# Global part of the values product in two 64-row tiles, its values masked within a head group, and batch 1's first transposes in the score pair

## The chip, the cores and the metric

The kernel runs on one core of a Trainium2 chip. The core has five engines that run side by side, each with its own queue of instructions in program order: TensorE (PE; its weight loads are listed as PEld), VectorE (DVE), ScalarE (ACT), GpSimd (POOL) and SyncE (SP). SP and POOL issue most of the DMAs; sixteen DMA engines carry them out. [...] The metric is the device time of one execution in microseconds, as the median of several runs.

## The reference

Attention with a band and eight global positions, on 8 batches, 8 heads, 576 positions and 64 elements a head, then a gated feed-forward block on the 4608 resulting tokens.

```python
def _attn_ref(q, k, v, global_idx):
    scores = scale * np.matmul(q, k.transpose(0, 1, 3, 2))
    pos = np.arange(S)
    mask = np.abs(pos[:, None] - pos[None, :]) <= window      # window = 32
    is_global[global_idx] = True                              # 8 positions
    mask = mask | is_global[:, None] | is_global[None, :]
    scores = np.where(mask, scores, -1000000000.0)
    attn = softmax(scores)
    return np.matmul(attn, v)
...
def _moe_ref(x, w_gate, w_val, w_out):
    g = x @ w_gate
    silu = g * (1.0 / (1.0 + np.exp(-g)))
    return (silu * (x @ w_val)) @ w_out
```

Here x is the attention output with the heads side by side (4608 x 512), the gate and value weights are 512 x 1536, the output weights 1536 x 512.

## The kernel before

**Attention of one batch.** It is a row of steps, all within `attention(b)`. `step_T` (lines 363 to 387; batch 0 has its own, `step_T0`) transposes k and q of a pair of heads with PE into one PSUM pair and copies them to kT and qT; batches 3 and up get kT and qT from DMA transposes on SP instead, whose sources are bf16 copies made by POOL's casting DMAs (`cast_qk`, tiles kf and qf). `step_GT` transposes the gathered, masked rows of the global positions. `step_S2` and `step_SG` make the scores of the global queries against all keys and of all queries against the global keys; the latter, exponentiated and masked, are the tile pg: 128 partitions, 16 for each head, by 576 positions. `step_P2T` transposes the global queries' probabilities to p2t: with PE and an ACT copy up to batch 3, with a DMA transpose on SP from batch 4 on (line 448). `step_AV2` (line 458) multiplies them with the values va. Its result has, in every partition, two heads' columns (66 wide: 64 values, the sum and a low part); DVE spreads it with the mask dmask into the tile gv, in which each of the eight heads has its columns and only that head's partitions are not zero (lines 468 to 480).

`step_S` (line 482) makes banded scores: matmuls with 64 rows (one head) and 128 columns, two of them, in different row halves of the array, into two banks. ACT exponentiates, DVE multiplies with the band. `step_AV` (line 532) adds up, for 128 positions, a group of four heads in each of two banks: for each group first the global part, two matmuls with all 128 partitions of pg as rows, 64 positions as columns each, and the 264 columns of gv of that group (line 546), then eight windowed matmuls with 64 columns (line 555) on va and on its shifted copy vb, a DMA on SP. `normalise` on DVE divides, and `step_X` transposes the result into xT. `step_AV8` (line 566) does the same for the last 64 positions, both groups in one bank.

**The feed-forward block** works in nine chunks of 512 tokens. Each chunk has twelve gates (eight 128x128 matmuls of 512 columns each, then tanh on ACT and two products on DVE, gv and h) and four output steps (twelve matmuls each, a copy on ACT, a DMA out). These 16 units per chunk set the order: every step of attention is hung behind a unit by hand (`gaps`), batch b + 1 beside the units of chunk b for most of the kernel, and each engine executes in that order.

**PSUM** has eight banks: the score pair (pool psc, tag "sc", two banks), a second pair (pool pm, tag "m") and four single banks (pool pf) for gates and outputs. A pair is handed over only when its last reader is done. Gate 2 of chunk 0 also takes the pair "m" (pgv).

Batch 1's `step_T(0)` stands behind gate 2 of chunk 0, `step_T(1)` behind gate 3 (after batch 0's `step_AV8`), `step_T(2)` behind gate 4, `step_GT` and `step_T(3)` behind gate 5. In batches 3 to 7 the list of steps is spread over a chunk's units: score step 1 stands behind gate 6, score step 2 and `step_AV2` behind gate 8, score step 3 and `step_AV(0)` behind gate 9, score step 4 and `step_AV(2)` behind an output step, `step_AV(3)` and `step_AV8` behind a later one.

Of the kernel before, what the change touches and what calls it, by code (L numbers as in the profile page):

```python
# [9 lines left out]
FP32 = mybir.dt.float32  # L10
BF16 = mybir.dt.bfloat16
# [3 lines left out]
ALU = mybir.AluOpType  # L15
AX = mybir.AxisListType

P = 128


def bc(ap, dims):

    return bass.AP(tensor=ap.tensor, offset=ap.offset, ap=[ap.ap[0]] + dims)
# [3 lines left out]
def kernel(  # L27
# [11 lines left out]
    nc = tc.nc  # L39

    B, H, S, D = q.shape
# [8 lines left out]
    HP = H // 2  # L50
# [6 lines left out]
    W = D + 2  # L57
# [4 lines left out]
    const = ctx.enter_context(tc.tile_pool(name="const", bufs=1))  # L62
# [3 lines left out]
    bp = ctx.enter_context(tc.tile_pool(name="bp", bufs=2))  # L66
    gw = ctx.enter_context(tc.tile_pool(name="gw", bufs=2))
    work = ctx.enter_context(tc.tile_pool(name="work", bufs=2))
# [3 lines left out]
    psc = ctx.enter_context(tc.tile_pool(name="psc", bufs=1, space=bass.MemoryType.PSUM))  # L72
    pm = ctx.enter_context(tc.tile_pool(name="pm", bufs=1, space=bass.MemoryType.PSUM))
# [97 lines left out]
    def clear(i):  # L171
        nc.vector.memset(kT_bufs[i][:, :, 0:WIN], 0.0)
        nc.vector.memset(kT_bufs[i][:, :, WIN + S : KC], 0.0)
        nc.vector.memset(va_bufs[i][:, :, :, D : D + 2], 0.0)
        nc.vector.memset(va_bufs[i][:, :, :, D : D + 1], 1.0)
        nc.vector.memset(va_bufs[i][0:WIN, 0, :, :], 0.0)
        nc.vector.memset(va_bufs[i][P - WIN : P, 4, :, :], 0.0)
# [4 lines left out]
        out=oh16.rearrange("p h a r -> p (h a r)"),  # L182
# [4 lines left out]
        out=p8, in_=ident.rearrange("p (a g) -> p g a", g=NG), axis=AX.X, op=ALU.add  # L187
    )
    dmask = const.tile([P, HP, 2], FP32)
    gofs = const.tile([P, B], I32)  # L190

    nc.vector.tensor_tensor(out=dmask, in0=oh16[:, :, 0, :], in1=oh16[:, :, 1, :], op=ALU.add)
    clear(0)
    tmp8h = const.tile([P, NG], FP32)
    hrow = const.tile([P, 1], FP32)
    nc.vector.tensor_tensor(
        out=tmp8h, in0=dmask.rearrange("p h r -> p (h r)"), in1=i8_f, op=ALU.mult
# [4 lines left out]
        out=gidx_f, in_=gidx_i64.bitcast(I32).rearrange("p (a b) -> p a b", b=2)[:, :, 0]  # L202
# [8 lines left out]
        out=hrow, in0=hrow, scalar1=float(S), scalar2=gcol, op0=ALU.mult, op1=ALU.add  # L211
# [4 lines left out]
        out=mka, in_=oh16.rearrange("p h a r -> p a r h"), axis=AX.X, op=ALU.add  # L216
# [6 lines left out]
        out=thr, in0=asel, scalar1=R2 + 0.25, scalar2=-0.25, op0=ALU.mult, op1=ALU.add  # L223
# [114 lines left out]
    def attention(b):  # L338
        kT = kT_bufs[b % 2]
        va = va_bufs[b % 2]  # L340
        st = {}
# [21 lines left out]
        def step_T(hp):  # L363
            if hp == 0:
                qTs[b] = bp.tile([P, HP, S], BF16, tag="qT", name="qT")
            pool, tag = (pm, "m") if (hp in (0, 2) if b == 1 else hp == 3) else (psc, "sc")
            pair = pool.tile([P, 2, 1024], BF16, tag=tag, name="ps_t")
            pss = []
            for n, name in enumerate(("k", "q")):
                ps = pair[:, n, 0:S].rearrange("p (j i) -> p j i", j=LJ)  # L370
                pss.append(ps)
                src = loaded[b][name]
                for j in range(LJ):
                    for par in range(2):
                        nc.tensor.transpose(  # L375
                            out=ps[64 * par : 64 * par + 64, j, :],
                            in_=src[:, 2 * hp + par, D * j : D * (j + 1)],
                            identity=ident[0:LP, 0:LP],
                        )
            nc.scalar.copy(  # L380
                out=kT[:, hp, WIN : WIN + S].rearrange("p (i j) -> p i j", j=LJ),
                in_=pss[0].rearrange("p j i -> p i j"),
            )
            (nc.scalar.copy if hp % 2 else nc.vector.tensor_copy)(
                out=qTs[b][:, hp, :].rearrange("p (i j) -> p i j", j=LJ),
                in_=pss[1].rearrange("p j i -> p i j"),
            )
# [70 lines left out]
        def step_AV2():  # L458
            ps = mtile([P, 2, W], FP32, "ps_av2")
            for u in range(5):  # L460
                for hp in range(HP):
                    nc.tensor.matmul(
                        out=ps[32 * hp : 32 * hp + 32, :, :],
                        lhsT=st["p2t"][:, u, 32 * hp : 32 * hp + 32],
                        rhs=va[:, u, 2 * hp : 2 * hp + 2, :],
                        start=(u == 0), stop=(u == 4), skip_group_check=True,
                    )
            gv = bp.tile([P, HP, 2, W], BF16, tag="gv", name="gvt")
            nc.vector.tensor_tensor(  # L469
                out=gv, in0=bc(ps, [[0, HP], [W, 2], [1, W]]),  # L470
                in1=bc(dmask, [[2, HP], [1, 2], [0, W]]), op=ALU.mult,
            )
            lo = work.tile([P, HP, 2], FP32, tag="lo", name="lo")
            nc.vector.tensor_tensor(
                out=lo, in0=bc(ps[:, :, D : D + 1], [[0, HP], [W, 2]]), in1=dmask, op=ALU.mult
            )
            nc.vector.tensor_tensor(  # L477
                out=gv[:, :, :, D + 1], in0=lo, in1=gv[:, :, :, D], op=ALU.subtract
            )
            st["gv"] = gv  # L480
# [53 lines left out]
        def step_AV(tp):  # L534
            st["xa", tp] = work.tile([P, H, D], BF16, tag="xa", name="xa", bufs=3)
            if b == 0:
                pool, tag = (pm, "m") if tp % 2 else (psc, "sc")
            elif b < XQ:
                pool, tag = (psc, "sc") if tp and (b < XB or tp % 2) else (pm, "m")
            else:  # L540
                pool, tag = pm, "m"
            full = pool.tile([P, 2, 512], FP32, tag=tag, name="ps_av")
            ps = full[:, :, 0 : 4 * W].rearrange("p g (h c) -> p g h c", c=W)
            for hg in range(2):
                for e in range(2):
                    nc.tensor.matmul(  # L546
                        out=ps[64 * e : 64 * e + 64, hg],
                        lhsT=st["pg"][:, P * tp + 64 * e : P * tp + 64 * e + 64],
                        rhs=st["gv"].rearrange("p h r c -> p (h r) c")[:, 4 * hg : 4 * hg + 4, :],
                        start=True, stop=False, skip_group_check=True,  # L550
                    )
                pt = st["p", 2 * (tp // 2) + hg]
                for hl in range(4):
                    for e in range(2):
                        nc.tensor.matmul(  # L555
                            out=ps[64 * e : 64 * e + 64, hg, hl, :],
                            lhsT=pt[:, hl % 2, 4 * (hl // 2) + 2 * (tp % 2) + e, :],
                            rhs=(va if e == 0 else st["vb"])[:, tp, 4 * hg + hl, :],
                            start=False, stop=(hl == 3), skip_group_check=True,
                        )  # L560
            if b == 0:
                st["xa*", tp] = lambda: normalise(ps, st["xa", tp], 8)
            else:
                normalise(ps, st["xa", tp], 8)

        def step_AV8():
            pt = st["p", 4]
            if b >= XQ:
                full = psc.tile([P, 2, 512], FP32, tag="sc", name="ps_av8")
                ps = full[:, 0, 0 : 4 * W].rearrange("p (h c) -> p h c", c=W)  # L570
            else:
                ps = mtile([P, 4, W], FP32, "ps_av8")
            for hg in range(2):
                nc.tensor.matmul(
                    out=ps[64 * hg : 64 * hg + 64], lhsT=st["pg"][:, 512:576],
                    rhs=st["gv"].rearrange("p h r c -> p (h r) c")[:, 4 * hg : 4 * hg + 4, :],
                    start=True, stop=False, skip_group_check=True,
                )
            for hl in range(4):
                for hg in range(2):  # L580
                    h = 4 * hg + hl
                    nc.tensor.matmul(
                        out=ps[64 * hg : 64 * hg + 64, hl, :],
                        lhsT=pt[:, h % 2, h // 2, :], rhs=va[:, 4, h, :],
                        start=False, stop=(hl == 3), skip_group_check=True,
                    )
            st["xa8"] = work.tile([P, 4, D], BF16, tag="xa8", name="xa8")
            normalise(ps, st["xa8"], 4)
# [87 lines left out]
        if b < XQ:  # L676
# [7 lines left out]
            [L(step_S2), L(step_SG)],  # L684
            [L(step_S, 0), L(step_P2T)],
            [],
            [L(step_S, 1)],
            [L(step_S, 2), L(step_AV2)],
            [L(step_S, 3), L(step_AV, 0), L(step_X, 0)],
            [L(step_AV, 1), L(step_X, 1)],  # L690
            [L(step_S, 4), L(step_AV, 2), L(step_X, 2)],
# [187 lines left out]
```

The softmax here doesn't subtract the row's maximum and nothing guards it: scores larger than these inputs give would overflow.

## Time and profile before

| what | value |
|---|---|
| median of 6 runs | 370.38 us (367.71 to 371.48) |
| the profiled execution | 368.02 us |
| its span, first to last instruction | 366.3 us |
| PE clock granted, mean | 1.000 |
| L546 PE, global part of AV, 128x264 on 64 columns, x128 | 18.0 us busy, 295 ns each |
| L555 PE, windowed part, 128x66 on 64 columns, x512 | 35.4 us busy, 198 ns each |
| L493 PE, banded scores, 64x64 on 128 columns, x576 | 16.2 us busy, 196 ns each |
| L574 PE, global part of AV 8, x16 | 2.3 us busy, 284 ns each |
| L469 DVE, mask product gvt, 128x528, x8 | 5.6 us busy, 701 ns each |
| L448 SP, DMA transpose p2t, x4, issue to landing | 2.7 / 6.3 / 9.6 us (least, median, most) |

The span is that of one profiled execution on the core; its time includes 1.7 us before and after it. Busy time of PE counts pipelined matmuls that overlap, and their ends are modelled: how long a stretch of PE takes is read from the starts of its matmuls, not from their durations. A few matmul records are missing from the trace. A wait is put down to the engine whose event came last.

### The profile page before, as it was taken

Reading aid. Unit: us, or ns where it says so; the run is one execution under the profiler, and the core shown is the slowest. Engines: PE = TensorE matmul, PEld = TensorE weight load, DVE = VectorE, ACT = ScalarE, POOL = GpSimd, SP = SyncE. Lnnn points to the kernel's source line nnn. Section 1 sums busy time; section 2 is a strip of 40 time slices with the busy share of each in tenths; the row PEclk is TensorE's granted clock in tenths of the full one; section 3 lists DMA queues with packets and bytes.
Section 4 is the critical chain, followed back from the end, with each engine's and each line's share of the span. In section 5 each row is a group of like instructions: output and inputs, shape, how many; then the busy total and the mean of one; then the engine's idle time right before and its main releaser. Section 6 shows DMA issues by size and latency. Waiting matters only on the chain.

```text
span 366.3 us, 7940 instructions
## 1 busy us (share of the span) xinstructions
PE 345.7 (94%) x3237; PEld 175.2 (48%) x3290; DVE 235.7 (64%) x469; ACT 152.8 (42%) x237; POOL 96.7 (26%) x114
## 2 busy tenths in 40 slices
PE   3876999999999999999999999999999999999996
PEld 2554545554544454444444454444544454444444
DVE  6674787268944885488548854886388728824850
ACT  5634673467323552355225532552354323323322
POOL 7934545924444001450246013100000000000000
PEclk9999999999999999999999999999999999999999
DMA  7999999999999926999999999941340131011002
GB/s 104 143 215 204 125 201 195 184 197 142 152 174 159 181 55 113 117 153 158 151 137 142 157 124 146 180 66 53 108 100 2 43 113 27 0 57 60 0 9 108
DMA packets 141637, 43.52 MB, mean 119 GB/s; under 512 B 126368, under 2 KB 135840, under 8 KB 141600
## 3 DMA queue, kind: packets, MB, share of 16 engines
q0 software_dynamic: 93824, 19.40, 66.1%
q1 hardware_dynamic: 47776, 23.60, 31.2%
q8 instruction: 26, 0.43, 0.5%
q14 instruction: 11, 0.09, 0.1%
HBM read 38.28 MB, written 15.34 MB: 146 GB/s over the span
## 4 chain that ended last, share of the span: by engine, by line
PE 84%; DMA 6%; POOL 3%; DVE 3%; ACT 2%; issue 1%; POOLq 0%; DVEq 0%
PE po L772 25%; PE pg L711 24%; PE pv L711 23%; DMA kg<-in_k_dram,gofs 3%; DMA wg_sb<-in_moe_w_gate_dram 3%; PE ps_av L546 3%; PE ps_s L493 3%; PE ps_av L555 2%; ACT pe L501 1%; POOL va L102 1%; PE ps_t L375 1%; DVE pt L507 1%; DVE gvt L469 1%; PE ps_s L427 1%; PE po L759 1%
## 5 line engine op out<-in xcount | busy, mean ns | idle before, releaser
L711 PE MATMUL pg<-xT,wg_sb 128*128 128x512 bf16 x391 | 106.1, 380 | 1.9 <-issue 0.2
L711 PE MATMUL pv<-xT,wv_sb 128*128 128x512 bf16 x410 | 105.9, 379 | 0.2
L744 DVE SCALAR_TENSOR_TENSOR gv<-th,pg 128x512 bf16<-128x512 bf16 x107 | 73.2, 685 | 39.5 <-ACT th L742 38.8
L742 ACT ACTIVATE th<-pg 128x512 bf16<-128x512 f32 x107 | 63.9, 598 | 80.4 <-PE pg L711 76.3
L772 PE MATMUL po<-wo_sb,h 128*128 128x512 bf16 x409 | 92.6, 379 | 1.4 <-issue 1.0
L748 DVE TENSOR_TENSOR h<-gv,pv 128x512 bf16<-128x512 bf16 x107 | 73.5, 687 | 11.5 <-PE pg L711 0.5
L711 PEld LDWEIGHTS <-wv_sb 128*128 128x128 bf16 x424 | 41.5, 98 | 50.0
L772 PEld LDWEIGHTS <-h 128*128 128x128 bf16 x420 | 39.9, 98 | 46.4
L102 POOL DMA_DIRECT2D va<-in_v_dram x40 | 35.2, 976 | 97.3 <-PE ps_av L555 74.5
L711 PEld LDWEIGHTS <-wg_sb 128*128 128x128 bf16 x424 | 37.0, 98 | 40.9 <-issue 1.7
L777 ACT ACTIVATE osb<-po 128x512 f32<-128x512 f32 x35 | 20.9, 597 | 81.7 <-PE po L772 74.9
L501 ACT ACTIVATE pe<-ps_s 128x1024 bf16<-128x1024 f32 (+1 forms) x40 | 37.5, 938 | 18.7 <-PE ps_s L493 17.9
L507 DVE TENSOR_TENSOR pt<-pe,band 128x1024 bf16<-128x1024 bf16 (+1 forms) x40 | 25.4, 635 | 20.4 <-ACT pe L501 20.4
L522 DVE TENSOR_REDUCE den<-ps_av 128x8 f32<-128x16 f32 (+1 forms) x40 | 6.7, 167 | 35.6 <-PE ps_av L555 33.4
L528 DVE TENSOR_TENSOR xa<-ps_av,den 128x512 bf16<-128x512 f32 (+1 forms) x40 | 25.5, 638 | 1.7 <-DMA xT<-xa 0.3
L493 PEld LDWEIGHTS <-kT 64*128 64x128 bf16 x576 | 11.3, 98 | 15.9 <-issue 14.8
L546 PE MATMUL ps_av<-gvt,pg 128*64 128x264 bf16 x128 | 18.0, 295 | 0.9 <-DVE gvt L477 0.9
L555 PE MATMUL ps_av<-vb,pt 128*64 128x66 bf16 x256 | 17.7, 198 | 0.0
L555 PE MATMUL ps_av<-va,pt 128*64 128x66 bf16 x256 | 17.7, 198 | 0.0
L555 PEld LDWEIGHTS <-pt 128*64 128x64 bf16 x512 | 17.6, 114 | 0.2
L493 PE MATMUL ps_s<-qT,kT 64*128 64x64 bf16 x576 | 16.2, 196 | 1.1 <-ACT pe L501 1.1
L109 POOL DMA_DIRECT2D qf<-in_q_dram x5 | 14.0, 2804 | 0.0
(122 smaller groups left out, 220.9 us busy)
## 6 DMA issues: line engine op xcount, KB each, us to landing
out_dram<-osb SPq DMA_DIRECT2D x35, 256.0 KB, 2.1
vb<-va SPq DMA_DIRECT2D x14, 264.0 KB, 5.1
va<-in_v_dram POOLq DMA_DIRECT2D x24, 128.0 KB, 5.7
kf<-in_k_dram POOLq DMA_DIRECT2D x5, 576.0 KB, 11.6
qf<-in_q_dram POOLq DMA_DIRECT2D x5, 576.0 KB, 18.2
k_bf<-in_k_dram POOLq DMA_DIRECT2D x6, 288.0 KB, 13.6
q_bf<-in_q_dram POOLq DMA_DIRECT2D x6, 288.0 KB, 14.4
va<-in_v_dram POOLq DMA_DIRECT2D x16, 96.0 KB, 5.6
```

Source lines behind the costliest of these rows:

```text
L102: nc.gpsimd.dma_start(out=va[lo:hi, u, :, 0:D], in_=vs[t0 + lo : t0 + hi])
L493: nc.tensor.matmul(out=ps[:, par, 64 * slot : 64 * slot + 64], lhsT=kT[r : r + 64, hp, 64 * t : 64 * t + P], rhs=qTs[b][r : r + 64, hp, 64 ...
L501: nc.scalar.activation(out=pe, in_=ps[:, :, 0 : 64 * ns].rearrange("p r (s c) -> p r s c", c=64), func=AF.Exp, scale=SCALE,)
L507: mult = lambda: nc.vector.tensor_tensor(out=pt.rearrange("p r s c -> p (r s) c"), in0=pe.rearrange("p r s c -> p (r s) c"), in1=bc(band, ...
L528: nc.vector.tensor_tensor(out=xa.rearrange("p (g h) d -> p g h d", g=g), in0=bc(ps, pst + [[1, D]]), in1=bc(den, [[4, g], [1, 4], [0, D]]) ...
L546: nc.tensor.matmul(out=ps[64 * e : 64 * e + 64, hg], lhsT=st["pg"][:, P * tp + 64 * e : P * tp + 64 * e + 64], rhs=st["gv"].rearrange("p h ...
L555: nc.tensor.matmul(out=ps[64 * e : 64 * e + 64, hg, hl, :], lhsT=pt[:, hl % 2, 4 * (hl // 2) + 2 * (tp % 2) + e, :], rhs=(va if e == 0 els ...
L711: nc.tensor.matmul(out=ps[:, 0:n], lhsT=w[:, cc, P * fc : P * (fc + 1)], rhs=xT[:, cc, t0 : t0 + n], start=(cc == 0), stop=(cc == NCC - 1),)
L742: nc.scalar.activation(out=th[:, 0:n], in_=pg[:, 0:n], func=AF.Tanh, scale=0.5)
L744: nc.vector.scalar_tensor_tensor(out=gv[:, 0:n], in0=th[:, 0:n], scalar=1.0, in1=pg[:, 0:n], op0=ALU.add, op1=ALU.mult,)
L748: nc.vector.tensor_tensor(out=st["h"][:, fc, 0:n], in0=gv[:, 0:n], in1=pv[:, 0:n], op=ALU.mult)
L772: nc.tensor.matmul(out=po, lhsT=st["h"][:, fc, P * ts : P * (ts + 1)], rhs=wo_sb[:, fc, :], start=(fc == 0), stop=(fc == NFC - 1),)
```

## The change

The global part of the values product is split by head groups instead of by positions. Partitions 0 to 63 of pg belong to heads 0 to 3, partitions 64 to 127 to heads 4 to 7. One matmul for each group now takes its 64 partitions as rows and all 128 positions as columns; the two lie in different row halves and write different banks. gv is masked only within a group: it holds four heads' columns instead of eight, with a mask dmh that is made once at the start from dmask. In `step_AV` both global matmuls now come first, and the windowed matmuls of both groups after them. In `step_AV8` the two global matmuls take 64 rows and 64 columns each and write one bank, at different partitions.

Batch 1's `step_T(0)` takes the score pair instead of the pair "m", and its copy of q is made by ACT instead of DVE. In batches 3 to 7 `step_AV2` moves from behind score step 2 to behind score step 1.

```diff
@@ -190,6 +190,8 @@
     nc.vector.tensor_tensor(out=dmask, in0=oh16[:, :, 0, :], in1=oh16[:, :, 1, :], op=ALU.add)
+    dmh = const.tile([P, 2, 2], FP32)
+    nc.vector.tensor_tensor(out=dmh, in0=dmask[:, 0:2], in1=dmask[:, 2:4], op=ALU.add)
     clear(0)
@@ -363,7 +365,7 @@
-            pool, tag = (pm, "m") if (hp in (0, 2) if b == 1 else hp == 3) else (psc, "sc")
+            pool, tag = (pm, "m") if hp == (2 if b == 1 else 3) else (psc, "sc")
@@ -381,7 +383,7 @@
-            (nc.scalar.copy if hp % 2 else nc.vector.tensor_copy)(
+            (nc.scalar.copy if hp % 2 or (b == 1 and hp == 0) else nc.vector.tensor_copy)(
@@ -465,14 +467,14 @@
-            gv = bp.tile([P, HP, 2, W], BF16, tag="gv", name="gvt")
+            gv = bp.tile([P, 2, 2, W], BF16, tag="gv", name="gvt")
             nc.vector.tensor_tensor(
-                out=gv, in0=bc(ps, [[0, HP], [W, 2], [1, W]]),
-                in1=bc(dmask, [[2, HP], [1, 2], [0, W]]), op=ALU.mult,
-            )
-            lo = work.tile([P, HP, 2], FP32, tag="lo", name="lo")
+                out=gv, in0=bc(ps, [[0, 2], [W, 2], [1, W]]),
+                in1=bc(dmh, [[2, 2], [1, 2], [0, W]]), op=ALU.mult,
+            )
+            lo = work.tile([P, 2, 2], FP32, tag="lo", name="lo")
             nc.vector.tensor_tensor(
-                out=lo, in0=bc(ps[:, :, D : D + 1], [[0, HP], [W, 2]]), in1=dmask, op=ALU.mult
+                out=lo, in0=bc(ps[:, :, D : D + 1], [[0, 2], [W, 2]]), in1=dmh, op=ALU.mult
             )
@@ -542,13 +544,13 @@
             for hg in range(2):
-                for e in range(2):
-                    nc.tensor.matmul(
-                        out=ps[64 * e : 64 * e + 64, hg],
-                        lhsT=st["pg"][:, P * tp + 64 * e : P * tp + 64 * e + 64],
-                        rhs=st["gv"].rearrange("p h r c -> p (h r) c")[:, 4 * hg : 4 * hg + 4, :],
-                        start=True, stop=False, skip_group_check=True,
-                    )
+                r = slice(64 * hg, 64 * hg + 64)
+                nc.tensor.matmul(
+                    out=ps[:, hg], lhsT=st["pg"][r, P * tp : P * tp + P],
+                    rhs=st["gv"][r].rearrange("p h r c -> p (h r) c"),
+                    start=True, stop=False, skip_group_check=True,
+                )
+            for hg in range(2):
                 pt = st["p", 2 * (tp // 2) + hg]
@@ -572,8 +574,8 @@
             for hg in range(2):
                 nc.tensor.matmul(
-                    out=ps[64 * hg : 64 * hg + 64], lhsT=st["pg"][:, 512:576],
-                    rhs=st["gv"].rearrange("p h r c -> p (h r) c")[:, 4 * hg : 4 * hg + 4, :],
+                    out=ps[64 * hg : 64 * hg + 64], lhsT=st["pg"][64 * hg : 64 * hg + 64, 512:576],
+                    rhs=st["gv"][64 * hg : 64 * hg + 64].rearrange("p h r c -> p (h r) c"),
                     start=True, stop=False, skip_group_check=True,
                 )
@@ -684,8 +686,8 @@
             [],
-            [L(step_S, 1)],
-            [L(step_S, 2), L(step_AV2)],
+            [L(step_S, 1), L(step_AV2)],
+            [L(step_S, 2)],
             [L(step_S, 3), L(step_AV, 0), L(step_X, 0)],
```

## The prediction

> **What bounds the kernel now.** First the head of the page and its table of busy time: one engine sets the end.
>
> ```profile
> span 366.3 us, 7940 instructions
> PE 345.7 (94%) x3237; PEld 175.2 (48%) x3290; DVE 235.7 (64%) x469; ACT 152.8 (42%) x237; POOL 96.7 (26%) x114
> ```
>
> TensorE (PE) is busy for 94% of the span, and the chain that ended last is 84% PE. From about 36 us on its matmuls follow one another almost without a hole, so whatever PE is given or spared there moves the end one for one. VectorE (DVE, 64%) and ScalarE (ACT, 42%) have room. The change must then be read in three places: PE's own time in a step, the few waits of PE, and transfers that PE would meet earlier. Second, the list of waits; PE has few that this change touches:
>
> ```profile
> PE ps_t L375 <- DVE h L748: 2.5, 1, 2.5
> ...
> PE ps_av L546 <- DVE gvt L477: 0.9, 5, 0.2
> ```
>
> Once, 2.5 us: the first transposes of batch 1 wait for h of gate 2, which shares their PSUM pair. Five times, 0.2 us each: the global part of AV 0, in batches 3 to 7, waits for the masked values. Third, the timeline of PE around one AV step (start, duration):
>
> ```profile
> 253.06 0.30 PE L546 MATMUL ps_av<-gvt,pg 128*64 128x264 bf16 x2
> 253.20 0.19 PE L555 MATMUL ps_av<-va,pt 128*64 128x66 bf16 x1
> ...
> 253.33 0.28 PE L546 MATMUL ps_av<-gvt,pg 128*64 128x264 bf16 x2
> 253.44 0.19 PE L555 MATMUL ps_av<-va,pt 128*64 128x66 bf16 x1
> ...
> 253.54 0.19 PE L555 MATMUL ps_av<-vb,pt 128*64 128x66 bf16 x1
> 253.67 0.39 PE L772 MATMUL po<-wo_sb,h 128*128 128x512 bf16 x1
> ```
>
> Durations overlap, so starts are what to read. A pair of 64-column global matmuls costs 0.11 us (253.33 to 253.44) and runs side by side; right after a change of tile shape the same pair costs 0.14 (253.06 to 253.20). Eight windowed matmuls (four pairs) take 0.13. The last pair, 0.03, is followed by 0.10 of nothing before the 128x128 matmul at 253.67: that is a **change of shape**. It shows again here:
>
> ```profile
> 256.36 0.29 PE L493 MATMUL ps_s<-qT,kT 64*128 64x64 bf16 x8
> 256.58 0.30 PE L546 MATMUL ps_av<-gvt,pg 128*64 128x264 bf16 x2
> ...
> 247.44 0.41 PE L493 MATMUL ps_s<-qT,kT 64*128 64x64 bf16 x16
> 248.04 0.30 PE L546 MATMUL ps_av<-gvt,pg 128*64 128x264 bf16 x2 [0.19 <-DVE gvt L477]
> ...
> 169.74 0.41 PE L493 MATMUL ps_s<-qT,kT 64*128 64x64 bf16 x16
> 170.08 0.47 PE L462 MATMUL ps_av<-va,p2t 128*32 128x132 bf16 x20
> ```
>
> Score matmuls have just the shape that the change gives the global part: 64 rows, 128 columns, two at a time into two banks. Eight of them to the next step take 0.22, sixteen take 0.34 (169.74 to 170.08): so four pairs cost 0.12, one pair 0.03, which is the time of one matmul alone (264 columns take 0.11, so 64 take 0.03), and the rest of 0.22, 0.10, is the change of shape. The sixteen before AV 0 take 0.60 instead of 0.34: there PE really waits 0.26.
>
> **The change, part by part** (plus is gained).
>
> *1. Transposes of batch 1.* Gate 2's eight matmuls end at 32.40 (31.54 and four of 0.216). Step T 0 could start at 32.50; it starts at 35.08. In the score pair its last user is score step 4 of batch 0, read by an ACT exp at 30.85 to 31.45: no wait left. T 1 now follows in the same pair and must wait for T 0's two copies, both on ACT: first copy 0.74 after T 0's start (as now, 35.08 to 35.82), then 0.64 and 0.65, done near 34.5; PE reaches T 1 after T 0 (0.63), gate 3 (1.73) and AV 8 (0.23), near 35.1. Hidden, by 0.6. The ACT copy also holds up gate 3's tanh by some 0.1, hidden because gate 4 uses other banks. So 2.58 is won at 32.5, and the stall goes to what is late next: transfers, which do not come earlier.
>
> ```profile
> 40.87 0.39 POOL L247 TENSOR_TENSOR kqm<-qg,mka 128x128 bf16<-128x128 f32 x1
> 46.70 0.46 SPq L130 DMA_DIRECT2D vb<-va  x1
> DMA to landing us min/median/max: 7.6/7.6/7.6
> ```
>
> The gathered rows of batch 1 are masked until 41.26, so step GT, now at 42.74, cannot start before 41.3: 1.4 remains. The shifted values vb of batch 1, issued at 46.70, land 7.6 later, at 54.30; their first use in AV 0 is at 55.55 and becomes 54.35 at best: 1.20 remains. The new mask dmh adds one DVE operation (dmask's row: 0.16) ahead of the clears and of the gather's offsets, for which POOL waits; in the first 40 us the DMA engines are full, so I let landings slip by 0.15. **+1.05** (bounds: 0, if the loads are later still; 2.58, if they are earlier).
>
> *2. AV steps.* Removed: one global pair, 0.11, and the 0.03 of the first pair after a change. Added: a change of shape between the two parts, 0.10, and about 0.01 of refill, as score steps show. Net +0.03 each; AV 1 to 3 of batch 1 and four in each of batches 2 to 7, 27 in all, **+0.81**; AV 0 of batch 1, waiting for vb, saves its second pair, **+0.11**. Bounds per step: +0.06 if refills cost nothing, -0.08 if the row pair runs in series.
>
> *3. Score step straight before AV.* Both now have one shape: the change in front goes, 0.10. AV 0 and AV 2 of batches 3 to 7, AV 0 of batch 2: 11 times, **+1.10**. Bound below: 0.
>
> *4. Masked values ready earlier.* AV 2 (step_AV2) moves from score step 2 to score step 1, two gates earlier (it issues no DMA), so AV 0's wait goes: 5 x 0.26, **+1.30**. The smaller mask product saves DVE 0.27 (701 ns for 528 columns; 424 for 256 in xa), off the path. Behind it on DVE stand gate 7's products; two gates later there is one product less before score step 3's. No loss.
>
> *5. AV 8.* Its two matmuls become 64x64 tiles.
>
> ```profile
> 262.95 0.19 PE L555 MATMUL ps_av<-vb,pt 128*64 128x66 bf16 x1
> 262.98 0.28 PE L574 MATMUL ps_av<-gvt,pg 128*64 128x264 bf16 x2
> 263.09 0.29 PE L582 MATMUL ps_av<-va,pt 128*64 128x66 bf16 x8
> ```
>
> Today there is no change of shape on either side; two come in, 0.20 in batches 3 to 7, and 0.08 net in batches 1 and 2, where a gate precedes: **-1.16**. No 64x64 tile is in this trace: above, 0 if it is no change of shape; below, a further 0.11 for each of seven if the two run in series. I take the middle: all other shape changes cost the same, and all other tile pairs run together.
> [...]
>
> *6. The new wait.* AV 2 reads p2t, for batches 4 to 7 a DMA transpose. Moved two gates up, it meets the landing.
>
> ```profile
> 157.80 2.78 SPq L448 DMA_TRANSPOSE p2t<-p  x1
> DMA to landing us min/median/max: 9.6/9.6/9.6
> ...
> 165.84 0.41 PE L493 MATMUL ps_s<-qT,kT 64*128 64x64 bf16 x16
> ```
>
> Batch 4: issued 157.80, landed 167.40; score step 1 starts at 165.84, AV 2 would start 0.34 later, at 166.18: **1.27 of waiting**. Batch 5 in the same way: issued 195.46, 9.1 to landing, 204.56; score step 1 at 203.40, AV 2 at 203.74: 0.87, both with 0.05 for the semaphore (h of gate 2 ends at 35.03, PE starts at 35.08). Batches 6 and 7 land after 2.7 and 3.4 us, over 4 us early. What differs is the cast of a later batch's k (issued 155.03, landing 11.6 later), which runs beside the first two. PE is in order: behind the waiting matmul stand gate 7 and, on DVE, the mask product and gate 7's products; nobody else is late. Cast and transpose both hang on AV 8 of the batch before, so the distance keeps. **-2.14** (bounds: 0 if landing takes 8.3; -4 more if it takes two us longer each time).
> [...]
>
> **Sum:** 1.05 + 0.81 + 0.11 + 1.10 + 1.30 - 1.16 - 2.14 = +1.07. The profiled execution took 368.02 us (span 366.3 and 1.7 around it); the median shown is 370.38. So 366.95 for a run like the profiled one, and 369.3 for the median.
>
> **Rivals.** *A, no wait for p2t:* the transpose lands in time in most executions. For it: 1.3 us of earlier landing is enough, and 6 and 7 have far more. Against: both congested batches agree within 0.5. Gain 3.2, 367.2 us. *B, slower: the two row tiles run one after the other.* Each of 27 + 7 steps loses 0.11: 1.07 - 3.74 = -2.7, 373.1 us. It decides from 0.03 per pair (no gain left) and costs over 0.5% from 0.09. Against it stand the score pairs at 0.03 a pair. *C, p2t later:* with 11.6 instead of 9.6 in both batches, -4 more: 373.3 us; the old place was 2.6 and 3.0 from landing, so nothing in the trace shows more. *D, step 1 brings nothing*, since loads come later in slower executions: 370.4, inside "no change".
>
> **Numbers.** About 0.5% (1.85 us) is what can be told from no change. Forecast 0.60, A 0.25, B 0.07, C 0.08. Forecast alone: 368.0 to 371.2; of its 0.60, 0.05 gains over 0.5% (step 1 whole). So faster 0.30, same 0.55, slower 0.15. The range for 8 in 10 takes in A and the near part of C: 367.1 to 371.6.
>
> **What would show it.** Right: T 0 near 32.5 and holes before GT and the first vb; AV steps of 0.57 with one pair of 64x128 globals and a 0.10 gap behind it; no gap between scores and globals; holes of about 1.3 and 0.9 before AV 2 of batches 4 and 5, none in 6 and 7. Wrong: global starts 0.11 apart (B), no holes (A), or larger ones (C).

## The result, and the profile after

| | before | after |
|---|---|---|
| median | 369.6 us (74 runs, 367.49 to 375.37) | 367.15 us (37 runs, 365.38 to 370.01) |
| ratio | | 0.9936, 95% interval 0.9921 to 0.9952 |
| the profiled execution, its span | 368.02, 366.3 us | 366.57, 364.8 us |

The change makes the kernel faster by 0.64%, 2.4 us (1.8 to 2.9). Predicted was 369.3 us (367.1 to 371.6) from a gain of 1.07, "no change" the likeliest. The time lies in the range, but only 0.05 above its lower end, in part because the median before came out at 369.6, not at the 370.38 that the forecast started from (0.9936 of that is 368.0). The sign of the sum was right; its size was less than half, and by the forecast's own line of 0.5% the outcome is "faster", which had 0.30, not "no change", which had 0.55. The two profiles differ by 1.45 us, near the sum; the medians differ by more. That second difference is the case's question.

The head of the page and the waits of PE (engine, line, engine waited for; us in total, times, longest), after:

```profile
span 364.8 us, 7818 instructions
PE 346.6 (95%) x3177; PEld 170.8 (47%) x3226; DVE 233.7 (64%) x469; ACT 153.3 (42%) x238; POOL 97.4 (27%) x114
...
PE ps_av L464 <- DMA p2t<-p: 1.0, 2, 0.8
PE ps_g L395 <- POOL kqm L249: 0.8, 1, 0.8
```

PE sets the end as before (78% of the chain that ended last, 84% before). Both old waits are gone from the list (T 0 for h, AV 0 for the masked values); the two that take their place are those of the sum, for p2t and for the masked rows.

The timeline of all engines around the first transposes of batch 1 (start, duration, idle time in front and what ended it), after:

```profile
32.23 0.45 PE L377 MATMUL ps_t<-ident,k_bf 96*64 96x96 bf16 x12
...
40.84 0.40 POOL L249 TENSOR_TENSOR kqm<-qg,mka 128x128 bf16<-128x128 f32 x1
40.93 0.59 PE L395 MATMUL ps_g<-ident,kqm 128*128 128x128 bf16 x2 [0.77 <-POOL kqm L249]
...
54.32 0.22 PE L557 MATMUL ps_av<-vb,pt 128*64 128x66 bf16 x1
```

T 0 starts 2.85 us earlier (35.08 before). GT then waits 0.77 for the masked rows, and the first use of vb, 54.32 instead of 55.55, comes as its transfer lands (issued at 46.20, landed 8.08 later). 1.23 us are kept.

The timeline of PE around score step 3, AV 3 and AV 8 of batch 6, after:

```profile
246.47 0.41 PE L495 MATMUL ps_s<-qT,kT 64*128 64x64 bf16 x16
246.72 0.28 PE L548 MATMUL ps_av<-gvt,pg 64*128 64x264 bf16 x2
...
251.72 0.29 PE L548 MATMUL ps_av<-gvt,pg 64*128 64x264 bf16 x2
251.94 0.22 PE L557 MATMUL ps_av<-va,pt 128*64 128x66 bf16 x1
251.99 0.20 PE L557 MATMUL ps_av<-va,pt 128*64 128x66 bf16 x1
...
252.19 0.19 PE L557 MATMUL ps_av<-vb,pt 128*64 128x66 bf16 x1
252.32 0.39 PE L774 MATMUL po<-wo_sb,h 128*128 128x512 bf16 x1
...
261.48 0.19 PE L557 MATMUL ps_av<-vb,pt 128*64 128x66 bf16 x1
261.61 0.30 PE L576 MATMUL ps_av<-gvt,pg 64*64 64x264 bf16 x2
261.84 0.32 PE L584 MATMUL ps_av<-va,pt 128*64 128x66 bf16 x8
```

Sixteen score matmuls to the globals take 0.25 (in the profile before 0.60 in front of `step_AV(0)`, and 0.34 where only a change of shape follows); eight in front of `step_AV(2)` take 0.13 instead of 0.22: no change of shape, no wait. The globals to the windowed part take 0.22, a pair of 0.11 and a change of 0.10 or more; the next pair takes 0.05, where all others take 0.03. So an AV step is 0.60 (251.72 to 252.32) against 0.61 before; to the nanosecond it is 9 ns less. Around AV 8 there are now two changes, 0.10 (261.48 to 261.61 less the pair's 0.03) and 0.12 (261.61 to 261.84 less 0.11). The two matmuls of each `x2` start 3 or 4 ns apart in the trace, in AV 0 to 3 and in AV 8; matmuls that run one after the other start apart by their length (a gate's by 0.216).

The transposes of p2t on SP's queue, score step 1 and AV 2 of batch 4, then the same of batch 5, after:

```profile
156.19 1.57 SPq L450 DMA_TRANSPOSE p2t<-p  x1
...
164.23 0.41 PE L495 MATMUL ps_s<-qT,kT 64*128 64x64 bf16 x16
165.43 0.47 PE L464 MATMUL ps_av<-va,p2t 128*32 128x132 bf16 x20 [0.79 <-DMA p2t<-p]
...
202.40 0.41 PE L495 MATMUL ps_s<-qT,kT 64*128 64x64 bf16 x16
203.03 0.47 PE L464 MATMUL ps_av<-va,p2t 128*32 128x132 bf16 x20 [0.23 <-DMA p2t<-p]
```

Without a wait `step_AV2` (AV 2 from here on) would start 0.34 after the score step: it is 0.86 late in batch 4 and 0.30 late in batch 5.

A word on names: the earlier text puts score steps 1, 2 and 3 of batches 3 to 7 behind gates 6, 8 and 9. Counted from gate 0 they stand behind gates 7, 9 and 10. No number hangs on it.

### The profile page after: what moved, and what is told of

Its sections match the earlier page's. It is cut to its first block, busy times and chain, and to the rows that moved or that the text cites. A ratio compares the mean times of both kernels' runs of the same rounds, so it can differ in the third digit from the quotient of the medians.

```text
span 364.8 us, 7818 instructions
## 1 busy us (share of the span) xinstructions
PE 346.6 (95%) x3177; PEld 170.8 (47%) x3226; DVE 233.7 (64%) x469; ACT 153.3 (42%) x238; POOL 97.4 (27%) x114
## 4 chain that ended last, share of the span: by engine, by line
PE 78%; DMA 15%; POOL 3%; issue 2%; DVE 1%; ACT 1%; DVEq 0%; POOLq 0%
PE po L774 25%; PE pg L713 21%; PE pv L713 21%; DMA p2t<-p 5%; DMA kg<-in_k_dram,gofs 4%; DMA wg_sb<-in_moe_w_gate_dram 3%; PE ps_av L557 3%; PE ps_s L495 2%; DMA vb<-va 2%; POOL va L102 1%; PE ps_av L548 1%; DMA va<-in_v_dram 1%; PE po L761 1%; PE ps_av L464 1%; PE ps_t L377 1%
## 5 line engine op out<-in xcount | busy, mean ns | idle before, releaser
L713 PE MATMUL pv<-xT,wv_sb 128*128 128x512 bf16 x415 | 107.2, 379 | 0.3
L557 PE MATMUL ps_av<-va,pt 128*64 128x66 bf16 x256 | 14.9, 200 | 0.0
L557 PE MATMUL ps_av<-vb,pt 128*64 128x66 bf16 x256 | 14.6, 200 | 0.2
L109 POOL DMA_DIRECT2D kf<-in_k_dram x5 | 11.4, 2284 | 7.9 <-DMA qf<-in_q_dram 7.7
L557 PEld LDWEIGHTS <-pt 128*64 128x64 bf16 x512 | 11.2, 113 | 4.7 <-issue 0.5
```

Source lines behind the costliest of these rows:

```text
L109: nc.gpsimd.dma_start(out=t, in_=src[b].rearrange("h s d -> s h d"))
L557: nc.tensor.matmul(out=ps[64 * e : 64 * e + 64, hg, hl, :], lhsT=pt[:, hl % 2, 4 * (hl // 2) + 2 * (tp % 2) + e, :], rhs=(va if e == 0 els ...
L713: nc.tensor.matmul(out=ps[:, 0:n], lhsT=w[:, cc, P * fc : P * (fc + 1)], rhs=xT[:, cc, t0 : t0 + n], start=(cc == 0), stop=(cc == NCC - 1),)
```

## The experiments

Three groups of kernels, each measured beside the kernel before on the same chip. Its median there was 370.87, 369.53 and 369.55 us, so ratios are what to compare between groups. "Steady part" is the time in a profile from `step_GT` (GT) of batch 3 to the end: 250.06 us before, 249.94 after. "T 0" is batch 1's `step_T(0)`. The steady part leaves out the first 115 us, where loads come when they come.

### The first transposes, and what their wait costs

**e1: the kernel before, with the transposes' part of the change alone.**

```diff
-            pool, tag = (pm, "m") if (hp in (0, 2) if b == 1 else hp == 3) else (psc, "sc")
+            pool, tag = (pm, "m") if hp == (2 if b == 1 else 3) else (psc, "sc")
-            (nc.scalar.copy if hp % 2 else nc.vector.tensor_copy)(
+            (nc.scalar.copy if hp % 2 or (b == 1 and hp == 0) else nc.vector.tensor_copy)(
```

> Before with one part of the change alone: batch 1's first transposes in the score pair, their copy of q on ACT. Theory as in the prediction's step 1: PE starts these transposes near 32.5 instead of 35.08, then waits for the masked rows of batch 1 before GT (until about 41.3) and for vb before AV 0 of batch 1 (until about 54.3); 1.0 to 1.3 us are left of 2.6, ratio to before 0.997. Rival, since the two profiled executions differ by 1.45 us but the ratio of all runs says 2.4: in most executions this part is worth more, 2.0 to 2.5 us, ratio 0.994. Third: the transfers set the pace in most executions and nothing is left, ratio 1.000.

368.78 us, ratio 0.9938 (0.9909 to 0.9966): 2.3 us faster, as much as the whole change, not the 1.05 of the ledger (the sum of the prediction). Yet its profile holds what the ledger said. The waits of PE, e1:

```profile
PE ps_g L393 <- POOL kqm L247: 1.4, 1, 1.4
```

T 0 at 32.56, 1.4 of the 2.5 us given back before the masked rows, and AV 0 of batch 1 at 54.81 (55.41 before); the steady part is 250.08. This execution is even one of e1's longer ones (369.29): a wait of 1.1 near 77 us for a copy by ACT, which the profile before does not have, comes behind it. So the extra gain is in neither profile, and must be in what differs from one execution to the next.

**e3: the change without its transposes' part and with `step_AV2` in its old place.** Only the split is left.

```diff
-            pool, tag = (pm, "m") if hp == (2 if b == 1 else 3) else (psc, "sc")
+            pool, tag = (pm, "m") if (hp in (0, 2) if b == 1 else hp == 3) else (psc, "sc")
...
-            [L(step_S, 1), L(step_AV2)],
-            [L(step_S, 2)],
+            [L(step_S, 1)],
+            [L(step_S, 2), L(step_AV2)],
```

> Before with the split of the global part alone (row tiles, values masked within a group); first transposes of batch 1 and AV 2 where they were. Theory by the rows of the changed kernel: no change of shape between scores and AV (11 times 0.09), no wait of AV 0 (5 times about 0.2), two more changes of shape at AV 8 (5 times 0.21, 2 times 0.1), AV steps themselves level (0.01 each): 1.0 us faster, ratio 0.997. If the first transposes are worth 1.2 us, it lies 1.2 us above the kernel with AV 2 put back; if they are worth 2.4 us, 2.4 us above. Rival: the split is worth the larger share, 2 us, ratio 0.9945.

370.18 us, ratio 0.9999 (0.9966 to 1.0033), though its steady part is 0.94 shorter (249.12). Its profile happens to show what an execution can lose at the start. First the span and mean granted clock, then PE at its two long waits, then five stretches of the start (from and to, length; busy us of PE, PEld, DVE, ACT, POOL with instructions; granted clock; DMA share, GB/s), e3:

```profile
core 0: 371.6 us, clock 0.986
...
25.73 0.26 PE L557 MATMUL ps_av<-vb,pt 128*64 128x66 bf16 x1 [2.80 <-DMA vb<-va]
...
39.08 0.69 PE L377 MATMUL ps_t<-ident,k_bf 96*64 96x96 bf16 x12 [2.52 <-DVE h L750]
```

```profile
21.63:25.05 3.42, 1.07 (x8) 0.44 (x8) 2.05 (x5) 0.58 (x1) 0.79 (x2) 1.00 1.20 238
25.05:28.46 3.41, 2.73 (x40) 1.83 (x41) 1.07 (x3) 0.58 (x1) 1.62 (x2) 0.50 1.24 205
28.46:31.88 3.42, 3.42 (x20) 2.55 (x19) 1.07 (x3) 0.58 (x1) 1.31 (x3) 0.50 1.31 203
35.29:38.70 3.41, 1.28 (x6) 0.50 (x5) 3.26 (x6) 0.76 (x2) 0.23 (x1) 1.00 1.24 207
38.70:42.12 3.42, 3.04 (x29) 1.71 (x29) 1.08 (x2) 0.65 (x2) 0.77 (x3) 0.50 1.80 160
```

In this trace the granted clock changes at 25.05, 31.88, 38.70 and 42.12 us only, all on one grid of 3.41 us; the stretches above lie on it. Most of the wait for vb (22.93 to 25.73) falls into the first, most of T 0's (36.57 to 39.08) into the fourth, 2.1 us each. PE is busy for 31% and 37% of them, and in the next stretch **the clock is halved**, once for two stretches, once for one. Now the two stretches around T 0's wait in the profile before, laid on the same grid from its first clock record at 23.27 (in e3 25.05 is the first record, 18.22, and two such steps; in the profile before the next record, 368.01, is 101 steps behind the first):

```profile
30.10:33.51 3.41, 2.41 (x23) 1.21 (x22) 2.79 (x5) 1.95 (x4) 2.05 (x3) 1.00 1.31 205
33.51:36.92 3.41, 1.84 (x30) 1.17 (x30) 1.91 (x4) 0.77 (x2) 0.88 (x1) 1.00 1.24 204
```

The same wait, 32.57 to 35.08, is divided by a border of the grid into 0.9 and 1.6 us; PE is busy for 71% and 54%, and the clock stays at 1.00. f4, a second profile of the kernel before, is alike (1.1 and 1.4 us, 66% and 59%). T 0's wait is not the only one that half clock followed. f2 (below) has none, but its profile has a wait of 2.01 us for vb, from 23.70, within one stretch:

```profile
23.07:26.49 3.42, 1.25 (x26) 0.91 (x24) 1.51 (x6) 0.59 (x1) 1.06 (x1) 1.00 1.25 208
26.49:29.90 3.41, 3.41 (x35) 2.42 (x33) 1.87 (x5) 0.59 (x1) 1.40 (x2) 0.50 1.29 203
```

All 14 profiles say the same. Laid on each one's own grid, from its first clock record on, there are 1395 stretches at full clock. The five with PE busy for 37% or less (two of them at the very end of a kernel) were each followed by half clock; the others, all with 52% or more, by full clock. So where a wait falls on the grid goes with whether it costs a stretch of half clock, and that differs from execution to execution.

One such stretch lowers an execution's mean clock by 3.41 / 2 / 366, to 0.995, so the clock listed for every execution tells whether it had one. It does not tell what came before the first clock record (18.22 us in e3, 22.5 to 27.6 in the other thirteen profiles, 23.27 in the profile before): up to there pairs of score matmuls start 0.053 us apart, later 0.029, so PE was slower there by a factor of 1.8, uncounted, in the profiles whose mean is given as 1.000 too.

| kernels | executions with a mean clock below 0.9975 |
|---|---|
| T 0's wait there: before, in the three groups | 23 of 35, 18 of 35, 7 of 11 |
| T 0's wait there: before again (f4), split alone (e3) | 5 of 6, 6 of 12 |
| wait gone: after, e1, e2, e4 | 7 of 39, 3 of 12, 2 of 12, 0 of 12 |
| wait gone: e5, e6, e7, f1, f2, f3 | 1 of 12, 2 of 12, 1 of 12, 1 of 6, 1 of 6, 2 of 6 |

59 of 99 with the wait, 20 of 129 without it. (Of e8, whose added copies make new holes, 5 of 12.) An estimate agrees: if a wait of 2.51 us falls anywhere on the grid with equal chance, one stretch holds 2.0 us or more of it, as in f2, in (3.41 - 2.51 + 2 x 0.51) / 3.41, or 0.56, of the executions. Executions of before with the lower clock are longer by 1.4, 2.6 and 2.7 us in the three groups (medians 371.0 against 369.6, 370.58 against 367.96, 370.5 against 367.82); half of one stretch is 1.7. At full clock e1 stands at 368.29 against 369.60: 1.3 faster, the ledger's step. The rest is the clock: a share smaller by 0.44 (0.60 less 0.16), times 1.7 to 2.2 us (2.2 is the mean of those three), is an estimated 0.75 to 1.0 us.

**f4: the kernel before once more**, unchanged, to see how far two profiles of one kernel lie apart.

> The kernel before, unchanged, once more: a second profile of it and a control. Ratio 1.000 within 0.003. Theory: where its executions are longer than the first profiled one (368.0 us against a median of 369.6), the time lies in the first 115 us (a later first AV for want of vb of batch 0, the wait of the first transposes of batch 1 after it), and from GT of batch 3 to the end it again takes 250.1. Rival: the scatter lies in the later part, and GT of batch 3 to the end differs by more than 0.3.

370.1 us, ratio 1.0012 (0.9975 to 1.0048), span 366.0, and again a steady part of 250.06: that part repeats to 0.01, and scatter lies in front of it.

**e7: e1, and batch 1's gathered rows and first values loaded ahead of a weight.** The ledger had the transfers as the cap on this step.

```diff
-        load_wgv(2)
         g1 = gather(1)
         load_v(1, range(0, 3))
+        load_wgv(2)
```

> Before with the first transposes of batch 1 in the score pair (as in the first experiment), and in addition the gather of the global rows and the first three loads of va of batch 1 ahead of the last third of the gate and value weights. Theory: what caps that part's gain is the landing of batch 1's loads; the masked rows are ready some 3 us earlier, GT no longer waits (1.6 in the first experiment's profile), and vb lands earlier: 1.0 to 1.5 us faster than the first experiment, ratio to before 0.990. Rival: in most executions the start runs so late that these loads cap nothing, as the ratio of the first experiment (2.3 us of the 2.6) suggests: level with it, 0.993 to 0.995. Third: the weights become late for gates 8 to 11, a new wait, slower.

365.39 us, ratio 0.9901 (0.9866 to 0.9935). The timeline of PE at GT and AV 0 of batch 1, e7:

```profile
39.92 0.28 PE L393 MATMUL ps_g<-ident,kqm 128*128 128x128 bf16 x2
...
52.26 0.41 PE L493 MATMUL ps_s<-qT,kT 64*128 64x64 bf16 x16
52.59 0.30 PE L546 MATMUL ps_av<-gvt,pg 128*64 128x264 bf16 x2
52.73 0.19 PE L555 MATMUL ps_av<-va,pt 128*64 128x66 bf16 x1
52.73 0.19 PE L555 MATMUL ps_av<-vb,pt 128*64 128x66 bf16 x1
```

No wait before either; the span is 2.7 shorter than before, the whole of the 2.58 that T 0 wins. The loads were the cap, as the trace says; the ratio's interval overlaps e1's.

### The place of AV 2, and the late p2t

**e2: the change with `step_AV2` back behind score step 2** (the second hunk of e3's diff alone).

> The changed kernel with AV 2 (the values product of the global queries) put back behind score step 2. Theory: the smaller mask product (426 ns instead of 701) by itself has the masked values ready within 0.1 us of AV 0, so the waits of AV 0 do not come back; the waits for p2t (0.86 and 0.30 us in the profiled execution) go. The holes before AV 2 of batches 4 and 5 vanish, the gap before AV 0 is below 0.1, and the kernel is 0.9 to 1.9 us faster than the changed one: ratio to before 0.989 to 0.991. Rival, as the prediction's step 4 had it: the five waits of 0.26 return, 1.3 us, and the kernel is level with the changed one, 0.993 to 0.995.

368.94 us, ratio 0.9949 (0.992 to 0.9979), not to be told from the change's 0.9936. The steady part can be told: 249.14, 0.80 shorter than after. No wait for p2t, and before AV 0 a gap of only 0.06: the masked values come in time from the old place, since their product is smaller. The group of that product, after (busy, mean ns, idle before it):

```profile
L471 DVE TENSOR_TENSOR gvt<-ps_av,dmh 128x264 bf16<-128x264 f32 x8 | 3.4, 426 | 0.1
```

426 ns instead of 701. So the smaller product takes away 0.20 of the 0.26 by itself. **The move of AV 2 bought 0.06 us a batch and paid 1.16 in all.**

**e5: the change with `step_AV2` on its own one gate later**, between score steps 1 and 2.

```diff
-            [L(step_S, 1), L(step_AV2)],
+            [L(step_S, 1)],
...
+            [L(step_AV2)],
...
+        gaps[o + 8] = gaps.get(o + 8, []) + steps.pop()
```

> The changed kernel with AV 2 of batches 3 to 7 alone behind the gate that follows score step 1's, halfway between its old place and its new one. Theory: p2t has landed by then (0.5 to 0.9 us to spare by the two profiled executions), and the masked values are still ready before AV 0. No hole before AV 2 of batches 4 and 5, no gap before AV 0 (below 0.01); from GT of batch 3 to the end 248.8 us, against 249.9 in the changed kernel, 249.1 with AV 2 put back and 250.1 before. As a ratio to before 0.990 if the start is as in the changed kernel. Rival: an extra change of shape on both sides of AV 2, which now stands between two gates (0.10 in front instead of the change from scores, none saved), costs 0.1 in each batch: 249.3.

366.57 us, ratio 0.9934 (0.9903 to 0.9964); steady part 249.31 and no hole. One gate more is enough for the transpose, but AV 2 alone pays a change of shape of its own, some 0.1 a batch (an estimate from 249.31 where 248.8 was expected, over five batches).

**e6: the change with the casts of batches 6 and 7 issued later**, behind the first load of values that AV 0 releases.

```diff
-        if b > 4:
+        if b == 5:
             cast_at[b] = o - 32 + 8
-        v_at[b] = o - 16 + 2
+        if b < 6:
+            v_at[b] = o - 16 + 2
+        else:
+            at(o - 16 + 2, load_v, b, range(0, 1))
+            at(o - 16 + 2, cast_qk, b)
+            at(o - 16 + 2, load_v, b, range(1, 5))
```

> The changed kernel with the casts of k and q of batches 6 and 7 behind the first load of va that AV 0 of the batch before releases, some 20 us later, so that they no longer run beside the transposes p2t of batches 4 and 5. Theory: the cast is what makes p2t late. p2t of batches 4 and 5 lands 2.6 to 4 us after issue instead of 9.2 and 8.6, the holes of 0.86 and 0.30 before AV 2 vanish, and from GT of batch 3 to the end it takes 248.8 us. Rival: p2t of these batches waits for something else (the shifted values, kT's transposes, outputs): it lands after more than 8 us as before and the holes stay, 249.9. Cost to watch: transposes of the attention output now run beside the cast.

366.28 us, ratio 0.992 (0.9888 to 0.9952). The time from issue to landing of the four p2t transposes (least, median, most), after and then e6:

```profile
DMA to landing us min/median/max: 2.6/6.1/9.2
```

```profile
DMA to landing us min/median/max: 3.4/4.7/7.1
```

Batch 4's falls from 9.2 to 3.7 us: there the cast beside it made the transpose late. Batch 5's falls only from 8.6 to 7.1, and batch 6's rises from 2.6 to 5.8, with no cast beside either (the last one landed at 191.64 and 227.94, the transposes were issued at 194.26 and 231.57). What runs beside them is loads of values and gathers on POOL's queue, which stand behind the cast there and land until 199.64 and 234.93. So it is not the cast alone: these transposes were late (7.1 and 5.8) beside other transfers of POOL too, of which the casts are the largest (576 KB each, a load of values at most 128). In e8 (below), where the casts start later as well and none of them runs beside batches 4 and 5, both land after 2.6 us. Why 9.2 us beside the cast and 3.7 without it stays open. Steady part 249.22; a gate now waits 0.4 for a transfer of xT instead.

### AV 8 with 128 rows, to save its two changes of shape

All three need a second, fully masked gv for AV 8.

**e4: e2, with that gv as a second DVE product from PSUM.**

```diff
+            gv8 = bp.tile([P, HP, 2, W], BF16, tag="gv8", name="gvf")
+            nc.vector.tensor_tensor(
+                out=gv8, in0=bc(ps, [[0, HP], [W, 2], [1, W]]),
+                in1=bc(dmask, [[2, HP], [1, 2], [0, W]]), op=ALU.mult,
+            )
...
-                    out=ps[64 * hg : 64 * hg + 64], lhsT=st["pg"][64 * hg : 64 * hg + 64, 512:576],
+                    out=ps[64 * hg : 64 * hg + 64], lhsT=st["pg"][:, 512:576],
```

> As the kernel with AV 2 put back, and AV 8 with its global part as before the change (two matmuls of 128 rows and 64 columns), fed from a second tile masked over all eight heads, which costs DVE three more operations (0.70, 0.15 and 0.20 us) in each batch. Theory: two changes of shape less in batches 3 to 7 (5 times 0.21), one less in batches 1 and 2 (2 times 0.1), DVE's work hidden: 1.25 us faster than the kernel with AV 2 put back, ratio to before 0.986 to 0.988. Rival: DVE's 1.05 us more between score step 2 and AV 0 come in front of PE, since the second product delays what stands behind it: level with or slower than the kernel with AV 2 put back.

371.58 us, ratio 1.001 (0.9982 to 1.0038); steady part 251.32, 2.18 longer than e2's. The waits of PE, e4:

```profile
PE ps_av L561 <- DVE lof L489: 2.9, 5, 0.6
```

L561 is AV 0's global part. Its PSUM pair is the one AV 2 used, handed over only when AV 2's last reader is done, and the second product is that reader: the wait that e2 did not have comes back as 0.73 a batch.

**e8: e5, with that gv copied together by GpSimd from SBUF**, so that PSUM is free at once.

```diff
+    gv8_bufs = [const.tile([P, HP, 2, W], BF16, name=f"gv8{i}") for i in range(2)]
...
+            gv8 = gv8_bufs[b % 2]
+            for hg in range(2):
+                r = slice(64 * hg, 64 * hg + 64)
+                nc.gpsimd.tensor_copy(out=gv8[r, 2 * hg : 2 * hg + 2], in_=gv[r])
...
```

> As the kernel with AV 2 halfway, and AV 8's global part with 128 rows and 64 columns again; its values for all eight heads are put together by GpSimd, two copies of 64 partitions by 264 columns from the masked tile into one whose other blocks stay zero. Theory: AV 8 loses its two changes of shape (5 times 0.21), DVE and PSUM are untouched: from GT of batch 3 to the end 247.7 us, 1.1 less than with AV 2 halfway; ratio to before 0.987. In the experiment with a second DVE product the gap before AV 0 grew to 0.73 since AV 0's pair is handed over only when its last reader, that product, is done; here the pair has no new reader and the gap stays below 0.01. Rival: GpSimd's copies stand in front of its loads of va and gathers, and those come late.

368.62 us, ratio 0.9992 (0.9956 to 1.0029); steady part 250.77 against e5's 249.31. From GT of batch 5 to GT of batch 6, and from there to batch 7's, it is shorter, 37.17 us each against 37.41 in e5: **0.24 a batch is the price of AV 8's two changes** (0.22 by the rows above). But the copies wait on GpSimd for the masked values, and GpSimd's loads and casts wait behind them. The waits of PE, e8:

```profile
PE po L782 <- DVE h L758: 2.4, 1, 2.4
PE pg L721 <- DMA xT<-xa: 2.4, 2, 2.0
```

**f2: f1 (below), with the same copies on DVE.**

> As the one before, and AV 8's global part with 128 rows again; its values for all eight heads are put together by DVE, two copies of 64 partitions by 264 columns from SBUF (not from PSUM) into a tile whose other blocks stay zero. Theory: two changes of shape less at AV 8, 1.07 us less from GT of batch 3 to the end (248.1), ratio 0.9845; the gap before AV 0 stays near 0.06 since the pair in PSUM has no new reader. Rival: DVE's two copies, some 0.2 us each, delay the gate products behind them and PE waits for banks: 249 or more.

366.38 us, ratio 0.9924 (0.9888 to 0.996); steady part 249.66, 0.52 longer than f1's. The waits of PE, f2:

```profile
PE po L781 <- DVE h L757: 1.1, 6, 0.2
```

DVE, busy for 64% in the profile before, is not free at that place: behind the copies gate 11's h comes late for the first output step, once a batch, and from GT to GT a batch takes 37.48 us against 37.38 in f1, though AV 8's changes are saved. None of the three ways is a gain.

### Together

**f1: e2 with e7's order of loads; f3: the change with it.**

> The changed kernel with AV 2 put back behind score step 2 and with the loads of batch 1 ahead of the last third of the gate and value weights. Against the kernel with the first transposes and the early loads alone (ratio 0.990, executions within 1 us of each other) it has only the split more. Theory: the split saves 0.9 us from GT of batch 3 to the end (249.1 against 250.1 in the profiles) and this shows in the ratio once the start no longer scatters: 0.9875. Rival: the split brings nothing, as its own ratio of 1.000 (0.997 to 1.003) said, since it costs in the first 115 us what it saves later: 0.990.

> The changed kernel as it is, with the early loads of batch 1 alone added. Theory: the loads capped the changed kernel too (waits of 0.9 before GT and 0.3 before vb in its profile): 1.2 to 1.5 us less than its 0.9936, ratio 0.990; against the kernel with AV 2 put back it keeps the holes before AV 2 of batches 4 and 5, 249.9 from GT of batch 3 to the end. Rival: no cap in most of its executions, 0.993.

f1: 364.6 us, ratio 0.9888 (0.9845 to 0.993), span 363.6, steady part 249.14. f3: 366.09 us, ratio 0.9907 (0.987 to 0.9945), span 362.6, steady part 249.47 with holes of 0.31 and 0.38 for p2t. f1 is the fastest kernel of the study, 1.1% under before. The intervals of f1, f3 and e7 overlap: that the early loads help is shown by e7's trace, that the split adds anything to the *time* is not. At full clock f1's median is 0.92 under e7's (364.44, 365.36), as the steady parts say, but from two groups and five executions of f1. And e2 and e1, in one group, differ by the split as well: 368.94 and 368.78.

## Why the prediction came out as it did

**Step 1, T 0, +1.05: the step that was mis-sized.** As an account of one execution it held: T 0 at 32.23 for 32.5, 1.23 kept for 1.05, the loads named as the cap (e7). But the wait's price was taken from one profile whose clock stayed at 1.000. Of the executions with that wait about six in ten have the lower mean clock, of those without it fewer than two, and each such execution is 1.4 to 2.7 us longer: taking the wait away gave 2.3 us in e1 (1.3 to 3.4) where the term was 1.05. The page shown could have warned: five of the six times behind its median lie 1.0 to 3.5 us above the profiled 368.02. The median and the profile differed for a reason, and the sum was carried over from one to the other as if they did not.

**Step 2, AV steps, +0.81.** 0.60 for 0.57: the windowed part's first pair, too, takes longer after its change (0.05 for 0.03). Net 0.01 a step, some 0.3 for the 27.

**Step 3, scores before AV, +1.10.** As predicted: sixteen take 0.25 for 0.34, eight 0.13 for 0.22.

**Step 4, masked values earlier, +1.30.** The wait is gone, but credited to the wrong edit: the smaller product, costed "off the path", removes most of it alone (e2, 0.06 of 0.26 left). It was on the path, as AV 0 waited for just that.

**Step 5, AV 8, -1.16.** 0.24 a batch (e8 against e5), 0.20 predicted. The two 64x64 tiles start 3 ns apart in one bank.

**Step 6, p2t, -2.14.** Its place was right, its cause, the cast, for batch 4 (e6); it cost 1.16, as batch 4 landed after 9.2 and batch 5 after 8.6 (9.6 and 9.1 in the profile before). From issue to score step 1 it is 8.04 us as before, so each tenth of landing time moves the wait by a tenth; its bounds had said so.

**Steps 2 to 6 together** were to give 0.02, and -0.24 of it in batches 3 to 7 (0.60 + 1.00 + 1.30 - 1.00 - 2.14); there the steady part gives 0.12. Where nothing waits for p2t a batch takes 37.30 us from GT to GT against 37.56, 0.26 less; five times that less 1.16 is the 0.12. The errors, 0.4 too much in step 2 and 1.0 too heavy a cost in step 6 above all, work against each other: that the sum came near the 1.45 of the two profiles is in part luck.

**Rivals.** A (no wait for p2t, 367.2) names the time measured, for a reason that isn't there: the waits exist, and e2, which has none, gains 0.80 in the steady part, too little to show in its ratio. B falls (3 ns), C falls (landings were shorter, not longer), D falls with e1.

**Open.** The split alone is worth 0.94 us in the trace and nothing that e3's ratio could tell from zero, to 0.3%. In e2's profile GT of batch 3 comes at 118.06, in the change's at 114.90, with the same steps in front: e2's masked rows are later (GT of batch 1 at 42.55 for 40.93), and it has the wait of 1.1 that e1 has near 77 us. What decides from execution to execution whether these come was not settled. Nor was the clock's drop provoked on purpose: that the wait causes it rests on the rows above and on the counts, with and without it. No profile of the kernel before fell on an execution with the lower clock, so whether the half clock there followed T 0's wait, or one for vb as in f2, was not seen. And when PE first runs at the faster pace (the first clock record, between 18.2 and 27.6 us in the profiles) differs from execution to execution too, stands in no listed mean and was not followed up.

## What to carry to other kernels

A wait of 2.51 us on a busy TensorE cost more than its length here, by chance (mean clock below 0.9975 in 59 of 99 executions with it, in 20 of 129 without): count the executions whose mean clock is below 1 before pricing it from one profile, above all where the profile lies at the low end of the times. Before moving a step to hide a latency, make the step's own work smaller and look again; here that was enough, and the move bought a new wait for a transfer. And a change of matmul shape cost 0.10 to 0.12 us here, and 0.02 more in the first pair behind it: look at both neighbours before giving a step a new shape.

## What was not expected of the hardware

The clock was halved after stretches of 3.41 us in which PE was still busy for 31% and 37% (e3, f2), and in none of the 14 profiles after one with 52% or more. And one DMA transpose of the same size landed after 2.6 us with no cast beside it and after 9.2 with one (batches 6 and 4 of the profile after), and after 7.1 beside loads and gathers alone (batch 5 of e6).
